# Cluster attention ahead of two expert layers: how ties are broken and who prepares a pair of heads

## The chip, the cores and the metric

The program runs on one core of a Trainium2 chip. The metric is the time of one execution on the device, in microseconds (us); lower is better. Three runs of the kernel before took 713.77 to 715.09 us, with a median of 714.46. The execution that the profiler recorded took 715.44 us, of which 713.6 are the span from the first instruction to the last. TensorE is called PE in the rows (PEld is its weight load), VectorE DVE, ScalarE ACT, GpSimd POOL, and SP is the engine that issues most DMAs.

## The reference

Three layers follow one another: attention with clusters, a layer with a PReLU, and a layer of eight experts. The change touches the first alone:

```python
q_assign = np.argmax(np.einsum('bhsd,hcd->bhsc', q_n, c_n), axis=-1)   # q_n, c_n: normalized
k_assign = np.argmax(np.einsum('bhsd,hcd->bhsc', k_n, c_n), axis=-1)
mask = q_assign[:, :, :, None] == k_assign[:, :, None, :]
scores = scale * np.matmul(q, k.transpose(0, 1, 3, 2))                 # scale = 1/8
scores = np.where(mask, scores, -1000000000.0)
scores = scores - np.max(scores, axis=-1, keepdims=True)
attn = np.exp(scores)
attn = attn / (np.sum(attn, axis=-1, keepdims=True) + 1e-09)
return np.matmul(attn, v).astype(np.float32)
```

There are 2 batches, 8 heads, 768 tokens of 64 numbers, and 16 clusters. `argmax` takes the first of equal maxima. A query sees the keys of its own cluster only.

## The kernel before

Attention goes over eight **pairs** of heads, n = 0 to 7 (four pairs for each batch). A head has six tiles of 128 queries, so a pair is twelve **steps**, k = 0 to 11, and `i = 12n + k` counts all 96. The order of the instructions is written out by hand: the strings `ORD` say for each third step in which order the parts follow, and every engine takes its instructions strictly in that order.

A step has these parts. `scores` (S): four matmuls give 128 x 768 scores; each is a product of a high part (`AB`) and a correction (`CD`), and `CD` also holds the one-hot of the cluster, with 2^60 where the key's cluster is the same, so that the mask is part of the product. `highest` (M): VectorE takes the maximum of each row. `expo` (E): ScalarE computes the exponential and, as a second output, the row's sum into `den`. `transp` (A, B): two steps later TensorE transposes the exponentials, ScalarE copies them as the high part `eth`, and VectorE subtracts for the low part `etl` (a, b). `pv` (P): the product with V, whose high and low parts stand beside each other in `vh`. `evac` (V) takes a finished group of three tiles from PSUM. `X` is one step of a conversion of the next layer's weights, spread over ScalarE (L585, L586), VectorE (L588, L590, L592) and GpSimd (L594); it stands at the steps that `CVX` does not exclude.

The next pair m = n + 1 is prepared inside the steps of pair n, at the end of the step:

- k = 1 and 2: `sims`, twelve small matmuls in all, give the similarity of 128 x 192 query (then key) and cluster values; VectorE takes the maximum (L193) and marks what equals it (L195). Rounding can mark two clusters. To keep the first, GpSimd multiplies the marks by weights 16 to 1 (`weigh`, L202), at k = 3 VectorE takes the maximum again (L211), and GpSimd turns it into one-hots in two instructions (L217, L218).
- k = 2 and 3: `split`, eight instructions of GpSimd, makes the high and low parts of queries and keys (`RL`). k = 6: `place` copies them to `AB` and `CD` by DMA.
- k = 8 (7 for m = 1): `onehots` transposes the one-hots on TensorE (L253), ScalarE copies them (L264, L265), and `placeoh` sends them to `CD` by three DMAs.
- k = 8: `load` of the pair after that; k = 8 and 10: `vsplit` of V, the high part by ScalarE (L246), the low part by GpSimd (L247). k = 11: `scaleq`, GpSimd multiplies the loaded queries by 1/8 (L226). For pair 1 ScalarE does so ahead of the loop (L223).

Every tile that TensorE writes here for transposes, similarities and one-hots comes from one pool of three PSUM buffers (`pt`). `recip` (L387, L388) adds 1e-9 to the sums and inverts them at k = 10 and at k = 1 of the next pair; GpSimd spreads the inverse (`rx`, L391), and TensorE transposes that two steps later (`pb`, L400). The scores' PSUM tile `s` has two buffers, so the scores of step i wait for the exponential of step i - 2.

Ahead of step 0 stands the preparation of pair 0, in its own code, with idle matmuls (`warm`, L141) between.

Of the kernel before, what the change touches and what calls it, by code (L numbers as in the profile page):

```python
# [8 lines left out]
F32 = mybir.dt.float32  # L9
F32R = mybir.dt.float32r  # L10
BF16 = mybir.dt.bfloat16
# [9 lines left out]
P = 128  # L21
B, H, S, D = 2, 8, 768, 64
NC_ = 16
# [70 lines left out]
OK = 8  # L94
CVX = (5, 6, 7, 8, 11)
REST = 4
SIM, SP, S2, VS = (1, 2), (2, 3), 3, (8, 10)
# [3 lines left out]
def attention(ctx, tc, A, cst, xs, Tp, conv=None, prepare=None, then=None):  # L101
# [75 lines left out]

    G = 2 * NT * 2
    halves = [slice(u * 384, (u + 1) * 384) for u in range(2)]

    def sims(n, x):
        b, p = seq[n]
        if x == 0:
            pairs[n] = hk.tile([P, G, NC_], F32, tag="eq", name="eq", bufs=1)
        eq = pairs[n]
        sim = ps_t.tile([P, 512], F32, tag="pt", name="sim")
        for t in range(NT):
            nc.tensor.matmul(sim[:, t * 32:(t + 1) * 32], lhsT=Tp[:, x, t * P:(t + 1) * P],
                             rhs=bd[:, p].rearrange("p j c -> p (j c)"), start=True, stop=True)
        g = G // 2  # L190
        sv = sim[:, :g * NC_].rearrange("p (g c) -> p g c", c=NC_)
        mx = wk.tile([P, g], F32, tag="mx", name="mx")
        nc.vector.tensor_reduce(out=mx, in_=sv, axis=AX.X, op=ALU.max)  # L193
        ex = eq[:, x * g:(x + 1) * g]
        nc.vector.tensor_tensor(out=sv if n == 0 else ex, in0=sv, in1=mx.unsqueeze(2).to_broadcast([P, g, NC_]), op=ALU.is_equal)  # L195
        if n == 0:
            weigh(nc.vector, ex, sv)
        elif x == 1:
            weigh(nc.gpsimd, eq, eq)

    def weigh(eng, out, eq):
        eng.tensor_tensor(out=out, in0=eq, in1=cw.unsqueeze(1).to_broadcast(eq.shape), op=ALU.mult)  # L202

    def sims2(n, xs=(0, 1)):
        eq = pairs[n]
        if xs[0] == 0:
            hots[n] = hk.tile([P, 2, NT, 32], BF16, tag="oh", name="oh", bufs=1)
        g = G // 2
        gs = slice(xs[0] * g, (xs[-1] + 1) * g)
        m2 = wk.tile([P, G], F32, tag="m2", name="m2")  # L210
        nc.vector.tensor_reduce(out=m2[:, gs], in_=eq[:, gs], axis=AX.X, op=ALU.max)  # L211
        oh, mb = hots[n].rearrange("p x t (j c) -> p (x t j) c", c=NC_)[:, gs], m2[:, gs].unsqueeze(2).to_broadcast([P, gs.stop - gs.start, NC_])
        if n == 0:
            nc.vector.tensor_tensor(out=oh, in0=eq[:, gs], in1=mb, op=ALU.is_equal)
        else:

            nc.gpsimd.tensor_tensor(out=eq[:, gs], in0=eq[:, gs], in1=mb, op=ALU.subtract)  # L217
            nc.gpsimd.tensor_scalar(out=oh, in0=eq[:, gs], scalar1=-1.0, scalar2=1.0, op0=ALU.max, op1=ALU.add)  # L218

    def scaleq(n):  # L220
        q = Tp[:, 0]
        if n == 1:
            nc.scalar.mul(q, q, 0.125)  # L223
        else:
            for u in halves:
                nc.gpsimd.tensor_scalar(out=q[:, u], in0=q[:, u], scalar1=0.125, scalar2=None, op0=ALU.mult)  # L226
# [14 lines left out]
    def vsplit(n, j):  # L241
        vt = loads[n]
        vh = wk.tile([P, NT, 2 * D], F32R, tag="vh", name="vh", bufs=4)
        vj = vt[:, j].rearrange("p (t d) -> p t d", d=D)
        h, l = (slice(0, D), slice(D, 2 * D))[::1 - 2 * j]
        nc.scalar.copy(vh[:, :, h], vj)  # L246
        nc.gpsimd.tensor_tensor(out=vh[:, :, l], in0=vj, in1=vh[:, :, h].bitcast(F32), op=ALU.subtract)  # L247
        heads[n, j] = vh
# [7 lines left out]
    def onehots(n):  # L256
        oh = hots.pop(n)
        po = ps_t.tile([P, 512], F32, tag="pt", name="po")
        for x in range(2):
            turn(oh, po, x)  # L260
        pv = po.rearrange("p (x g s) -> p x g s", x=2, g=2)
        st = hk.tile([96, 2, 2, P], F32R, tag="st", name="st", bufs=1)
        heads[n, "st"] = st
        nc.scalar.copy(st[:, 0], pv[:96, 0])  # L264
        nc.scalar.activation(st[:, 1], pv[:96, 1], AF.Copy, bias=-BIG, scale=BIG)  # L265
# [35 lines left out]
    def scores(i):  # L301
# [10 lines left out]
        if t % 3 == 0:  # L312
            if j == 0:
                dens[n, t // 3] = wk.tile([P, 2, 3], F32, tag="den", name="den", bufs=4)
# [12 lines left out]
    def expo(i):  # L327
# [4 lines left out]
                             accum_out=den[:, i % 3:i % 3 + 1])  # L332
# [52 lines left out]
    def recip(n, g):  # L385
        rd = wk.tile([P, 2, 3], F32, tag="rd", name="rd")
        nc.vector.tensor_scalar(out=rd, in0=dens[n, g], scalar1=1e-9, scalar2=None, op0=ALU.add)  # L387
# [58 lines left out]
    nc.gpsimd.memset(CDs[1][D:].bitcast(F32), 0.0)  # L446
    if len(seq) > 1:
        load(1)
        scaleq(1)
# [11 lines left out]
    for i in range(NI + L + 7):  # L461
# [55 lines left out]
        if m < len(seq):  # L517
            if k in SIM:
                sims(m, SIM.index(k))
            if k == S2 and m == 1:  # L520
                sims2(m)
            if k in SP:
                split(m, SP.index(k))
            if k == S2 and m > 1:
                sims2(m)
            if k == 6:
                place(m, 0)
            if k == (OK if m > 1 else OK - 1):
                onehots(m)
                placeoh(m, 0)  # L530
            if k == LK and m + 1 < len(seq):
                load(m + 1)
            if k == VS[0]:
                vsplit(m, 0)
            if k == VS[1]:
                vsplit(m, 1)
            if k == 11 and m + 1 < len(seq):
                scaleq(m + 1)
# [1355 lines left out]
```

## Time and profile before

| | us |
|---|---|
| median of three runs | 714.46 |
| lowest, highest | 713.77, 715.09 |
| profiled execution | 715.44 |
| its span | 713.6 |
| TensorE, share of the span busy | 694.8, 97% |
| VectorE | 573.5, 80% |
| ScalarE | 472.7, 66% |
| GpSimd | 379.0, 53% |

Attention is the first third of the span: the first scores start at 11.8 us, the last exponential at 245.7. Matmuls overlap each other, so a TensorE that reads as 97% busy can still be held up; what tells it apart is the distance from the scores of one step to those of the next.

### The profile page before, as it was taken

What the parts mean: (1) busy time and instruction counts of PE and PEld (TensorE: products, weight loads), DVE (VectorE), ACT (ScalarE), POOL (GpSimd) and SP (SyncE); (2) the same over time, 40 slices, a digit from 0 to 9 for tenths busy, and PEclk for the clock granted to TensorE, in tenths of its full rate; (3) what the DMA queues carried; (4) which work ended last, traced back from release to release, by engine and by line L of the source; (5) the groups of instructions that cost most, each with busy time, mean ns of one, the idle gap of its engine ahead of it and who ended that gap; (6) DMA issues with size and microseconds to landing.
All of it is one profiled execution on the core that took longest, in us unless ns stands there. A gap on an engine that the chain in (4) does not pass through costs nothing.

```text
span 713.6 us, 11822 instructions
## 1 busy us (share of the span) xinstructions
PE 694.8 (97%) x4111; PEld 623.9 (87%) x4111; DVE 573.5 (80%) x1145; ACT 472.7 (66%) x917; POOL 379.0 (53%) x339
## 2 busy tenths in 40 slices
PE   8999999999999999999999999999999999999995
PEld 6988989989999899888889999999888989898883
DVE  6989988898989878887884989977458888787871
ACT  6879788888889964445544655566645767564660
POOL 4649788697886386666663000001024888885101
PEclk9999999999999999999999999999999999999998
DMA  7867676666775133334303600016453999988000
GB/s 200 222 158 170 134 178 153 159 155 135 173 170 107 59 118 118 118 122 133 132 28 117 194 1 1 1 59 180 130 193 103 358 383 354 340 322 324 34 14 25
DMA packets 43905, 108.43 MB, mean 152 GB/s; under 512 B 8698, under 2 KB 24522, under 8 KB 38464
## 3 DMA queue, kind: packets, MB, share of 16 engines
q1 hardware_dynamic: 36768, 67.03, 34.4%
q0 software_dynamic: 7072, 40.60, 15.5%
q8 instruction: 34, 0.56, 0.3%
q14 instruction: 31, 0.25, 0.1%
HBM read 74.78 MB, written 10.10 MB: 119 GB/s over the span
## 4 chain that ended last, share of the span: by engine, by line
PE 68%; DVE 7%; DMA 7%; POOL 6%; ACT 5%; issue 5%; POOLq 0%; ACTq 0%; DVEq 0%
PE h L677 18%; PE y L726 16%; DMA raw<-in_wall_dram,wi 6%; PE yo L1210 6%; PE hw L1288 5%; PE pt L342 4%; PE h L1210 3%; PE s L308 2%; PE px L360 2%; PE y L736 2%; PE s L311 2%; DVE nm L324 2%; ACT e L331 2%; DVE etl L345 2%; PE px L362 2%
## 5 line engine op out<-in xcount | busy, mean ns | idle before, releaser
L345 DVE TENSOR_TENSOR etl<-pt,eth 128x384 fp32r<-128x384 f32 x192 | 102.0, 549 | 19.9 <-ACT eth L344 18.8
L344 ACT CAST eth<-pt 128x384 fp32r<-128x384 f32 x192 | 90.9, 486 | 21.0 <-PE pt L342 20.9
L1177 POOL DMA_INDIRECT xg<-y1d,gi x16 | 27.3, 1708 | 130.2 <-DVE gi L1026 113.8
L342 PE MATMUL pt<-ident,e 128*128 128x128 f32 x576 | 93.8, 273 | 0.3 <-ACT e L331 0.3
L331 ACT ACTIVATE e<-s,nm 128x768 f32<-128x768 f32 x96 | 87.4, 910 | 6.4 <-DVE nm L324 5.7
L324 DVE TENSOR_REDUCE nm<-s 128x1 f32<-128x768 f32 x96 | 90.4, 943 | 1.0 <-PE s L311 0.8
L705 ACT CAST gh<-gm 128x384 fp32r<-128x384 f32 x60 | 30.8, 514 | 81.7 <-DVE gm L703 58.5
L342 PEld LDWEIGHTS pt<-ident,e 128*128 128x128 f32 x576 | 73.7, 140 | 6.9 <-ACT e L331 0.5
L707 DVE TENSOR_TENSOR gl<-gm,gh 128x384 fp32r<-128x384 f32 x60 | 49.3, 822 | 25.7 <-ACT gh L705 25.1
L360 PE MATMUL px<-etl,vh 128*64 128x384 f32 (+1 forms) x192 | 65.7, 369 | 1.6 <-DVE etl L345 1.3
L308 PE MATMUL s<-AB 128*128 128x384 f32 x192 | 57.6, 381 | 2.5 <-ACT e L331 2.0
L577 POOL TENSOR_TENSOR pre<-ct,pre 128x512 int32<-128x512 int32 x26 | 37.2, 1450 | 35.8 <-DVE ct L575 35.8
L677 PE MATMUL h<-xh,wh 128*128 128x384 f32 x256 | 55.6, 338 | 0.6 <-DVE gm L700 0.4
L677 PE MATMUL h<-xh,wl 128*128 128x384 f32 x256 | 56.0, 339 | 0.0
L677 PE MATMUL h<-xl,wh 128*128 128x384 f32 x256 | 55.0, 336 | 0.0
L362 PE MATMUL px<-eth,vh 128*128 128x384 f32 x160 | 54.0, 338 | 0.0
L1612 DVE TENSOR_TENSOR wl<-raw,wh 128x2048 fp32r<-128x2048 f32 (+2 forms) x26 | 44.4, 1714 | 11.2 <-ACT wh L1608 9.8
L311 PE MATMUL s<-CD 128*128 128x384 f32 x192 | 49.2, 337 | 1.1 <-DVE CD L439 1.1
L677 PEld LDWEIGHTS h<-xh,wh 128*128 128x128 f32 x256 | 45.5, 188 | 3.3 <-DVE gm L700 0.5
L677 PEld LDWEIGHTS h<-xh,wl 128*128 128x128 f32 x256 | 44.6, 188 | 2.8 <-POOL wl L649 2.7
L677 PEld LDWEIGHTS h<-xl,wh 128*128 128x128 f32 x256 | 45.7, 188 | 0.0
L726 PE MATMUL y<-wh,gh 128*128 128x512 f32 x168 | 43.6, 394 | 0.0
(383 smaller groups left out, 1826.9 us busy)
## 6 DMA issues: line engine op xcount, KB each, us to landing
AB<-RL SPq DMA_DIRECT2D x31, 384.0 KB, 5.2
raw<-in_w_in_dram SPq DMA_DIRECT2D x16, 512.0 KB, 4.1
raw<-in_w_out_dram SPq DMA_DIRECT2D x16, 512.0 KB, 4.8
raw<-in_wall_dram SPq DMA_DIRECT2D x8, 1024.0 KB, 7.2
Tp<-in_qkT_dram SPq DMA_DIRECT2D x16, 384.0 KB, 3.9
CD<-RL SPq DMA_DIRECT2D x15, 384.0 KB, 7.4
raw<-in_wall_dram POOLq DMA_DIRECT2D x4, 1024.0 KB
vt<-in_v_dram SPq DMA_DIRECT2D x8, 384.0 KB, 6.6
```

The lines of the kernel that those rows point to most:

```text
L308: nc.tensor.matmul(s[:, u, :384], lhsT=AB[:, 0, t * P:(t + 1) * P], rhs=AB[:, 1, ks], start=True, stop=False)
L311: nc.tensor.matmul(s[:, u, :384], lhsT=CD[:, 0, t * P:(t + 1) * P], rhs=CD[:, 1, ks], start=False, stop=True)
L324: nc.vector.tensor_reduce(out=nm, in_=s[:, :, :384], axis=AX.XY, op=ALU.max, negate=True)
L331: nc.scalar.activation(e.rearrange("p (u c) -> p u c", u=2), s[:, :, :384], AF.Exp, bias=nm, accum_out=den[:, i % 3:i % 3 + 1])
L342: nc.tensor.transpose(pt[:, i2], e[:, kt * P:(kt + 1) * P], ident)
L344: nc.scalar.copy(eh, pt)
L345: lows[u] = lambda: nc.vector.tensor_tensor(out=etl[:, 3 * u:3 * u + 3, q * P:(q + 1) * P], in0=pt, in1=eh.bitcast(F32), op=ALU.subtract)
L360: nc.tensor.matmul(px[:m], lhsT=vh[:, kt, :m], rhs=etl[:, kt], start=False, stop=False)
L362: nc.tensor.matmul(px, lhsT=vh[:, kt, :], rhs=eth[:, kt], start=False, stop=(kt == NT - 1))
L677: nc.tensor.matmul(hs[c], lhsT=a[:, k * P:(k + 1) * P], rhs=x[:, k, c * HC:(c + 1) * HC], start=(k == 0 and i == 0), stop=(k == KD - 1 and ...
L726: nc.tensor.matmul(ys[gi * GT + t], lhsT=a[:, t * P:(t + 1) * P], rhs=w, start=(f == 0 and n == 0), stop=(gi == 0 and f == NF - 1 and n == 2))
L1210: nc.tensor.matmul(out, lhsT=l[:, k], rhs=r[:, k * DM:(k + 1) * DM], start=start and k == 0 and i == 0, stop=stop and k == 3 and i == len( ...
```

## The change

It has four parts. (1) Ties: the marks of all equal maxima go straight into the one-hot tile as bf16 (L200 now), and are transposed as they are at k = 3 (`equals`); VectorE copies them from PSUM to `eqt`. At k = 4 (`onehots`) one product for queries and one for keys with a constant matrix `clear` subtracts, for each cluster, the marks of the clusters ahead of it; what is above 0 is the first mark. ScalarE takes it for the queries (`Relu`), VectorE for the keys. The four instructions of `weigh` and `sims2` go, for all pairs but the first. `placeoh` moves to k = 6, ahead of `place`. (2) V's high part is made by GpSimd with an addition of zero, and `vsplit` of the first head moves from k = 8 to k = 1. (3) The queries are scaled behind the similarities, at k = 1, by a `tensor_tensor` with a tile that holds 1/8, for pair 1 too. (4) The sums lie in four fixed tiles, each sum beside a column that holds 1e-9; `recip` adds the two columns with a `tensor_reduce`. These tiles, 1/8 and `clear` are filled by GpSimd ahead of step 0.

```diff
--- before.py
+++ after.py
@@ -91,10 +91,10 @@
 LATE = 3
 WARM = (8, 3, 4, 9, 6)
 PREP = (33, 45)
-OK = 8
+OK = 4
 CVX = (5, 6, 7, 8, 11)
 REST = 4
-SIM, SP, S2, VS = (1, 2), (2, 3), 3, (8, 10)
+SIM, SP, EQ, VS = (1, 2), (2, 3), 3, (1, 10)
 ORD = ("SMAPXaBbE", "SMAPaVBXEb", "SAPXBMabE")
 
 
@@ -175,14 +175,19 @@
         CDs.append(cd)
     nc.gpsimd.memset(CDs[0][D:].bitcast(F32), 0.0)
 
+    sums = [hk.tile([P, 2, 3, 2], F32, name=f"den{i}") for i in range(4)]
+    eighth = one.tile([P, 1], F32, name="eighth")
+    clear = one.tile([96, 2, 96], BF16, name="clear")
+
     G = 2 * NT * 2
     halves = [slice(u * 384, (u + 1) * 384) for u in range(2)]
 
     def sims(n, x):
         b, p = seq[n]
+        if x == 0 and n == 0:
+            pairs[n] = hk.tile([P, G, NC_], F32, tag="eq", name="eq", bufs=1)
         if x == 0:
-            pairs[n] = hk.tile([P, G, NC_], F32, tag="eq", name="eq", bufs=1)
-        eq = pairs[n]
+            hots[n] = hk.tile([P, 2, NT, 32], BF16, tag="oh", name="oh", bufs=1)
         sim = ps_t.tile([P, 512], F32, tag="pt", name="sim")
         for t in range(NT):
             nc.tensor.matmul(sim[:, t * 32:(t + 1) * 32], lhsT=Tp[:, x, t * P:(t + 1) * P],
@@ -191,39 +196,23 @@
         sv = sim[:, :g * NC_].rearrange("p (g c) -> p g c", c=NC_)
         mx = wk.tile([P, g], F32, tag="mx", name="mx")
         nc.vector.tensor_reduce(out=mx, in_=sv, axis=AX.X, op=ALU.max)
-        ex = eq[:, x * g:(x + 1) * g]
-        nc.vector.tensor_tensor(out=sv if n == 0 else ex, in0=sv, in1=mx.unsqueeze(2).to_broadcast([P, g, NC_]), op=ALU.is_equal)
+        eq = sv if n == 0 else hots[n][:, x].rearrange("p t (j c) -> p (t j) c", c=NC_)
+        nc.vector.tensor_tensor(out=eq, in0=sv, in1=mx.unsqueeze(2).to_broadcast([P, g, NC_]), op=ALU.is_equal)
         if n == 0:
-            weigh(nc.vector, ex, sv)
-        elif x == 1:
-            weigh(nc.gpsimd, eq, eq)
-
-    def weigh(eng, out, eq):
-        eng.tensor_tensor(out=out, in0=eq, in1=cw.unsqueeze(1).to_broadcast(eq.shape), op=ALU.mult)
+            nc.vector.tensor_tensor(out=pairs[n][:, x * g:(x + 1) * g], in0=sv, in1=cw.unsqueeze(1).to_broadcast(sv.shape), op=ALU.mult)
 
     def sims2(n, xs=(0, 1)):
         eq = pairs[n]
-        if xs[0] == 0:
-            hots[n] = hk.tile([P, 2, NT, 32], BF16, tag="oh", name="oh", bufs=1)
         g = G // 2
         gs = slice(xs[0] * g, (xs[-1] + 1) * g)
         m2 = wk.tile([P, G], F32, tag="m2", name="m2")
         nc.vector.tensor_reduce(out=m2[:, gs], in_=eq[:, gs], axis=AX.X, op=ALU.max)
         oh, mb = hots[n].rearrange("p x t (j c) -> p (x t j) c", c=NC_)[:, gs], m2[:, gs].unsqueeze(2).to_broadcast([P, gs.stop - gs.start, NC_])
-        if n == 0:
-            nc.vector.tensor_tensor(out=oh, in0=eq[:, gs], in1=mb, op=ALU.is_equal)
-        else:
-
-            nc.gpsimd.tensor_tensor(out=eq[:, gs], in0=eq[:, gs], in1=mb, op=ALU.subtract)
-            nc.gpsimd.tensor_scalar(out=oh, in0=eq[:, gs], scalar1=-1.0, scalar2=1.0, op0=ALU.max, op1=ALU.add)
+        nc.vector.tensor_tensor(out=oh, in0=eq[:, gs], in1=mb, op=ALU.is_equal)
 
     def scaleq(n):
-        q = Tp[:, 0]
-        if n == 1:
-            nc.scalar.mul(q, q, 0.125)
-        else:
-            for u in halves:
-                nc.gpsimd.tensor_scalar(out=q[:, u], in0=q[:, u], scalar1=0.125, scalar2=None, op0=ALU.mult)
+        for u in halves:
+            nc.gpsimd.tensor_tensor(out=Tp[:, 0, u], in0=Tp[:, 0, u], in1=eighth.to_broadcast([P, S // 2]), op=ALU.mult)
 
     def split(n, part):
         if part == 0:
@@ -243,7 +232,10 @@
         vh = wk.tile([P, NT, 2 * D], F32R, tag="vh", name="vh", bufs=4)
         vj = vt[:, j].rearrange("p (t d) -> p t d", d=D)
         h, l = (slice(0, D), slice(D, 2 * D))[::1 - 2 * j]
-        nc.scalar.copy(vh[:, :, h], vj)
+        if n:
+            nc.gpsimd.tensor_tensor(out=vh[:, :, h], in0=vj, in1=zero.unsqueeze(2).to_broadcast([P, NT, D]), op=ALU.add)
+        else:
+            nc.scalar.copy(vh[:, :, h], vj)
         nc.gpsimd.tensor_tensor(out=vh[:, :, l], in0=vj, in1=vh[:, :, h].bitcast(F32), op=ALU.subtract)
         heads[n, j] = vh
 
@@ -253,16 +245,25 @@
             nc.tensor.matmul(po[:96, (2 * x + g) * P:(2 * x + g + 1) * P], lhsT=oh[:, x, 3 * g:3 * g + 3].rearrange("p t c -> p (t c)"),
                              rhs=identb, start=True, stop=True)
 
-    def onehots(n):
+    def equals(n):
         oh = hots.pop(n)
         po = ps_t.tile([P, 512], F32, tag="pt", name="po")
         for x in range(2):
             turn(oh, po, x)
-        pv = po.rearrange("p (x g s) -> p x g s", x=2, g=2)
+        eqt = hots[n] = hk.tile([96, 2, 2 * P], BF16, tag="eqt", name="eqt", bufs=1)
+        nc.vector.tensor_copy(eqt, po[:96].rearrange("p (x s) -> p x s", x=2))
+
+    def onehots(n):
+
+        eqt = hots.pop(n)
+        po = ps_t.tile([P, 2, 2 * P], F32, tag="pt", name="po")
+        for x in range(2):
+            nc.tensor.matmul(po[:96, x], lhsT=clear[:, x], rhs=eqt[:, x], start=True, stop=True)
+        pv = po.rearrange("p x (g s) -> p x g s", g=2)
         st = hk.tile([96, 2, 2, P], F32R, tag="st", name="st", bufs=1)
         heads[n, "st"] = st
-        nc.scalar.copy(st[:, 0], pv[:96, 0])
-        nc.scalar.activation(st[:, 1], pv[:96, 1], AF.Copy, bias=-BIG, scale=BIG)
+        nc.scalar.activation(st[:, 0], pv[:96, 0], AF.Relu)
+        nc.vector.tensor_scalar(out=st[:, 1], in0=pv[:96, 1], scalar1=0.0, scalar2=-BIG, op0=ALU.max, op1=ALU.add)
 
     def onehot0(x):
 
@@ -311,7 +312,7 @@
             nc.tensor.matmul(s[:, u, :384], lhsT=CD[:, 0, t * P:(t + 1) * P], rhs=CD[:, 1, ks], start=False, stop=True)
         if t % 3 == 0:
             if j == 0:
-                dens[n, t // 3] = wk.tile([P, 2, 3], F32, tag="den", name="den", bufs=4)
+                dens[n, t // 3] = sums[2 * (n % 2) + t // 3]
             den = dens[n, t // 3][:, j]
             eth = wk.tile([P, NT, 384], F32R, tag="eth", name="eth", bufs=2)
             etl = wk.tile([P, NT, 384], F32R, tag="etl", name="etl", bufs=2)
@@ -329,7 +330,7 @@
         den = grp[i // 3][0]
         e = es.pop("e") if i == 0 else wk.tile([P, S], F32, tag="e", name="e", bufs=3)
         nc.scalar.activation(e.rearrange("p (u c) -> p u c", u=2), s[:, :, :384], AF.Exp, bias=nm,
-                             accum_out=den[:, i % 3:i % 3 + 1])
+                             accum_out=den[:, i % 3, :1])
         es[i] = e
 
     def transp(i, u):
@@ -384,7 +385,7 @@
 
     def recip(n, g):
         rd = wk.tile([P, 2, 3], F32, tag="rd", name="rd")
-        nc.vector.tensor_scalar(out=rd, in0=dens[n, g], scalar1=1e-9, scalar2=None, op0=ALU.add)
+        nc.vector.tensor_reduce(out=rd, in_=dens[n, g], axis=AX.X, op=ALU.add)
         nc.vector.reciprocal(out=rd, in_=rd)
         rx = wk.tile([P, 3, 2, D], F32, tag="rx", name="rx", bufs=1)
         eng = nc.gpsimd if n < len(seq) - 1 else nc.vector
@@ -444,9 +445,19 @@
     vsplit(0, 0)
     vsplit(0, 1)
     nc.gpsimd.memset(CDs[1][D:].bitcast(F32), 0.0)
+    nc.gpsimd.memset(eighth, 0.125)
+
+    cq, ck = clear[:, 0], clear[:, 1]
+    nc.gpsimd.memset(cq, -1.0)
+    cb = cq.rearrange("p (b c) -> p b c", c=NC_)
+    nc.gpsimd.affine_select(out=cb, in_=cb, compare_op=ALU.is_gt, fill=0.0, base=0, pattern=[[NC_, 6], [1, NC_]], channel_multiplier=-1)
+    nc.gpsimd.affine_select(out=cb, in_=cb, compare_op=ALU.is_ge, fill=0.0, base=0, pattern=[[-NC_, 6], [0, NC_]], channel_multiplier=1)
+    nc.gpsimd.tensor_tensor(out=cq, in0=cq, in1=identb[:96, :96], op=ALU.add)
+    nc.gpsimd.tensor_scalar(out=ck, in0=cq, scalar1=BIG, scalar2=None, op0=ALU.mult)
+    for d in sums:
+        nc.gpsimd.memset(d, 1e-9)
     if len(seq) > 1:
         load(1)
-        scaleq(1)
 
     def before():
         for f in range(3):
@@ -515,27 +526,25 @@
             if spare and i > NI + NRM:
                 spare.pop(0)()
         if m < len(seq):
+            if k == VS[0]:
+                vsplit(m, 0)
             if k in SIM:
                 sims(m, SIM.index(k))
-            if k == S2 and m == 1:
-                sims2(m)
+            if k == SIM[0]:
+                scaleq(m)
             if k in SP:
                 split(m, SP.index(k))
-            if k == S2 and m > 1:
-                sims2(m)
+            if k == EQ:
+                equals(m)
+            if k == OK:
+                onehots(m)
             if k == 6:
+                placeoh(m, 0)
                 place(m, 0)
-            if k == (OK if m > 1 else OK - 1):
-                onehots(m)
-                placeoh(m, 0)
             if k == LK and m + 1 < len(seq):
                 load(m + 1)
-            if k == VS[0]:
-                vsplit(m, 0)
             if k == VS[1]:
                 vsplit(m, 1)
-            if k == 11 and m + 1 < len(seq):
-                scaleq(m + 1)
     for do in spare:
         do()
     return fill
```

On GpSimd, between the preparation of pair 0 and that of pair 1, stood before (`vh` is V's parts of pair 0, `CD_168` a zero that pair 0 needs at k = 6, the rest is pair 1):

```order
L247 TENSOR_TENSOR vh<-vt,vh 128x6x64 x2
L446 MEMSET CD_168 64x1536
L202 TENSOR_TENSOR eq<-eq,cw 128x384
L234 TENSOR_TENSOR RL<-Tp,zero 128x384 x4
L217 TENSOR_TENSOR eq<-eq,m_366 128x384
L218 TENSOR_SCALAR oh<-eq 128x384
```

and at the same place after (`den_170` to `den_173` are the tiles of the sums):

```order
L239 TENSOR_TENSOR vh<-vt,vh 128x6x64 x2
L447 MEMSET CD_168 64x1536
L448 MEMSET eighth 128x1
L451 MEMSET clear 96x96
L453 AFFINE_SELECT clear<-clear 96x96
L454 AFFINE_SELECT clear<-clear 96x96
L455 TENSOR_TENSOR clear<-clear,identb 96x96
L456 TENSOR_SCALAR clear<-clear 96x96
L458 MEMSET den_170 128x12
L458 MEMSET den_171 128x12
L236 TENSOR_TENSOR vh<-vt,zero 128x6x64
L239 TENSOR_TENSOR vh<-vt,vh 128x6x64
```

The tiles of the sums are filled behind two passes over V, one large memset and six instructions for the constants.

On ScalarE, steps 7 to 10 of pair 2, before:

```order
L331 ACTIVATE e,den<-s,nm 128x768
L264 CAST st<-po 96x256
L265 ACTIVATE st<-po 96x256
L246 CAST vh<-vt 128x6x64
L344 CAST eth<-pt 128x3x128
L585 ACTIVATE w32a<-raw_78 128x256
L586 ACTIVATE raw_78<-raw_78 128x256
L344 CAST eth<-pt 128x3x128
L331 ACTIVATE e,den<-s,nm 128x768
```

and the same stretch after:

```order
L332 ACTIVATE e,den_170<-s,nm 128x768
L345 CAST eth<-pt 128x3x128
L594 ACTIVATE w32a<-raw_78 128x256
L595 ACTIVATE raw_78<-raw_78 128x256
L345 CAST eth<-pt 128x3x128
L332 ACTIVATE e,den_171<-s,nm 128x768
```

Three instructions between two exponentials are gone; the exponential now names the fixed tile of its sum.

On TensorE, a step before has the four transposes of one-hots alone (here step 7 of pair 0):

```order
L342 MATMUL pt<-ident,e 128x128 x3
L253 LDWEIGHTS oh
L253 MATMUL po<-identb,oh 96x128
L253 LDWEIGHTS oh
L253 MATMUL po<-identb,oh 96x128
L253 LDWEIGHTS oh
L253 MATMUL po<-identb,oh 96x128
L253 LDWEIGHTS oh
L253 MATMUL po<-identb,oh 96x128
L308 MATMUL s<-AB_167 128x384 x2
```

After, steps 3 and 4 of pair 0 (the tail of the transposes, then the product one step later):

```order
L245 LDWEIGHTS oh
L245 MATMUL po<-identb,oh 96x128
L309 MATMUL s<-AB_165 128x384 x2
L312 MATMUL s<-CD_166 128x384 x2
L343 MATMUL pt<-ident,e 128x128 x6
L261 LDWEIGHTS clear
L261 MATMUL po<-eqt,clear 96x256
L261 LDWEIGHTS clear
L261 MATMUL po<-eqt,clear 96x256
L309 MATMUL s<-AB_165 128x384 x2
```

The same transposes stand four or five steps earlier, and two matmuls of 256 columns are added between the transposes of one step and the scores of the next.

## Rows read from the trace of the kernel before

**Rows 1.** The page, busy time by engine: us (share of the span) instructions

```profile
PE 694.8 (97%) x4111; PEld 623.9 (87%) x4111; DVE 573.5 (80%) x1145; ACT 472.7 (66%) x917; POOL 379.0 (53%) x339
```

**Rows 2.** Timeline, TensorE, scores of a step: start, duration (us), engine, line, [idle before]

```profile
39.44 0.60 PE L308 MATMUL s<-AB 128*128 128x384 f32 x2
44.63 0.59 PE L308 MATMUL s<-AB 128*128 128x384 f32 x2
...
93.33 0.60 PE L308 MATMUL s<-AB 128*128 128x384 f32 x2
96.08 0.62 PE L308 MATMUL s<-AB 128*128 128x384 f32 x2 [0.43 <-ACT e L331]
...
147.03 0.61 PE L308 MATMUL s<-AB 128*128 128x384 f32 x2
149.11 0.60 PE L308 MATMUL s<-AB 128*128 128x384 f32 x2
...
151.45 0.59 PE L308 MATMUL s<-AB 128*128 128x384 f32 x2
155.56 0.60 PE L308 MATMUL s<-AB 128*128 128x384 f32 x2
158.50 0.59 PE L308 MATMUL s<-AB 128*128 128x384 f32 x2
```

**Rows 3.** Timeline, GpSimd, start of the kernel

```profile
1.00 0.29 POOL masks.py:199 TENSOR_SCALAR_AFFINE_SELECT ident<-ident 128x128 f32<-128x128 f32 x1
...
12.50 2.71 POOL L247 TENSOR_TENSOR vh<-vt,vh 128x384 fp32r<-128x384 f32 x2 [3.92 <-ACT vh L246]
15.27 1.38 POOL L446 MEMSET CD<- 64x1536 f32 x1
```

**Rows 4.** Timeline, TensorE and ScalarE, the first two exponentials and scores behind them

```profile
14.65 1.42 PE L188 MATMUL sim<-bd,Tp 128*128 128x32 f32 x12
15.14 0.90 ACT L331 ACTIVATE e<-s,nm 128x768 f32<-128x768 f32 x1 [1.56 <-DVE nm L324]
...
16.19 0.62 PE L308 MATMUL s<-AB 128*128 128x384 f32 x2
```

**Rows 5.** Timeline, ScalarE, step 8 of pair 2

```profile
92.80 0.39 ACT L265 ACTIVATE st<-po 96x256 fp32r<-96x256 f32 x1
93.08 0.52 ACT L246 CAST vh<-vt 128x384 fp32r<-128x384 f32 x1
...
93.85 0.45 ACT L585 ACTIVATE w32a<-raw 128x256 int32<-128x256 uint16 x1
```

**Rows 6.** Lines L387, L211: VectorE, times, duration ns min/median/max, first and last start

```profile
L387 DVE TENSOR_SCALAR rd<-den x16: 151/223/935, 34.3 to 248.9; 128x6 f32<-128x6 f32 x16
...
L211 DVE TENSOR_REDUCE m<-eq x9: 353/541/543, 8.1 to 201.5; 128x24 f32<-128x384 f32 x7, 128x12 f32<-128x192 f32 x2
```

**Rows 7.** Groups by form, 100 to 240 us: busy us, mean ns | idle before

```profile
L387 DVE TENSOR_SCALAR rd<-den 128x6 f32<-128x6 f32 x9 | 3.4, 376 | 0.0
...
L594 POOL TENSOR_TENSOR w32a<-raw,w32a 128x256 int32<-128x256 int32 x5 | 3.7, 744 | 1.1 <-DVE raw L592 1.1
```

**Rows 8.** Timeline, VectorE, one-hots of pair 0 from PSUM

```profile
13.41 0.42 DVE L442 CAST st<-po 96x256 fp32r<-96x256 f32 x1
```

**Rows 9.** Waits of the weight load, 20 to 245 us: total us, times, longest

```profile
PEld s L308 <- ACT e L331: 4.8, 10, 0.7
PEld px L360 <- DVE etl L345: 3.7, 9, 0.9
PEld sim L188 <- POOL Tp L226: 1.7, 2, 1.3
PEld pb L400 <- POOL rx L391: 0.9, 2, 0.4
```

**Rows 10.** Timeline, TensorE, warm matmuls, early and later

```profile
1.50 2.44 PE L141 MATMUL warm<-warm 128*128 128x384 bf16 x7
...
9.09 1.63 PE L141 MATMUL warm<-warm 128*128 128x384 bf16 x9
```

## The prediction, made before the changed kernel ran

> **What bounds the kernel now.** I read the page first: TensorE is busy for 97% of the span, VectorE for 80%, ScalarE for 66%, GpSimd for 53% [rows 1]. A busy TensorE may still be held up, so I went on to the distances between the scores of successive steps in TensorE's timeline. An undisturbed step lasts 149.11 - 147.03 = 2.08 us; one with the four transposes of one-hots lasts 151.45 - 149.11 = 2.34 [rows 2]. That is TensorE's own rhythm: nothing that another engine saves makes such a step shorter. Other steps are longer, and the waits of the weight load between 20 and 245 us say on whom they wait: 4.8 us on exponentials, 3.7 on low parts, 1.7 on the scaled queries, 0.9 on the inverted sums, 11.1 in all [rows 9]. So relief of the other engines is worth some 11 us at the very most, while each instruction added to TensorE, and each wait put into its chain, counts in full. The later layers are not touched; I take it that they begin earlier or later by what attention gains or loses.
>
> **The first exponential gets a new wait.** It writes its sum into a fixed tile, and GpSimd fills that tile first. In the order of GpSimd the fill stands behind V's low parts of pair 0, which end at 12.50 + 2.71 = 15.21, behind the memset from 15.27 to 16.65 [rows 3], and behind six instructions for the constants. The first exponential starts at 15.14 now, and waits for VectorE alone [rows 4]. Of the six, the trace shows a select over 128 columns at 0.29 [rows 3] and an addition over 256 columns at 0.74 [rows 7]. I take 0.29 for each of the two selects, 0.4 for the addition and for the scaling of 96 columns (nearer to the small row), 0.1 to 0.2 for each of the three small fills, 0.4 together, and for five dependent starts the 0.06 that lies between 15.21 and 15.27: 0.58 + 0.8 + 0.4 + 0.3 = 2.1. The tile is filled at 18.7, and the exponential starts 3.6 us later than now. Below, with 0.29 for the four larger ones and nothing for the rest, it is 16.65 + 1.16 - 15.14 = 2.7; above, with 0.74 for the addition and the scaling, 0.29 for five and 0.36 of gaps, 4.8.
>
> Behind that exponential ScalarE holds the second one and all copies of the transposed tiles; TensorE's scores of step 2 need its PSUM buffer and start at 16.19 for that reason, 0.12 after the similarities end at 14.65 + 1.42 [rows 4]. Nothing hides the wait: behind those scores follow transposes, the second similarities and the scores of step 3, all on TensorE in order, with no slack to give the time back. VectorE and GpSimd may run ahead in it, but they aren't the bound. I count +3.6.
>
> **The product that breaks ties.** The four transposes only move from step 8 to step 3. Two matmuls of 256 columns are added for each of seven pairs. The trace has no such product; its nearest row is the four transposes of 128 columns, 512 columns for 2.34 - 2.08 = 0.26 us [rows 2]. The two products pass 512 columns too: 7 x 0.26 = +1.8. With half as many weights to load it may be half of that, 0.9; if the array waits once more for each, twice, 3.6. They wait for VectorE's copy of the transposes, with a whole step between.
>
> **What goes.** (a) The similarities of a pair no longer wait for scaled queries: 1.7 us [rows 9], nearly all in step 1 of pair 1, which lasts 44.63 - 39.44 = 5.19 where 2.08 + 1.42 would do [rows 2, 4]. Late next would be the load, which is issued five steps earlier: -1.7. (b) GpSimd has less in its queue ahead of the spread of the inverted sums, since the two instructions of the ties and one `vsplit` are gone from there, and its remaining work starts two steps earlier; of the two waits of 0.9 in all [rows 9] I count -0.6 (0 to 0.9). (c) At step 8 ScalarE had two copies of one-hots and V's high part, 0.39 + 0.52 and a first of about the same as the 0.39, in front of the conversion's 0.45 [rows 5]; the step from 93.33 to 96.08 lasts 2.75 for it, 0.67 too long [rows 2], and pair 6 has one more such step: -1.3. Where no conversion falls there, the same copies cost nothing today. (d) The addition of 1e-9 has six numbers in a row and takes 151 ns at best and 935 at worst, while a reduction from SBUF over 384 columns takes 541 to 543 at every time [rows 6]: the one is held up while GpSimd works, the other isn't. Nine additions take 3.4 us where 9 x 0.15 would be 1.4 [rows 7], so they lose 2.0 us between 100 and 240, and in pair 4 the whole of it lands in a step of 158.50 - 155.56 = 2.94, 0.86 too long [rows 2]. Over all pairs I count -1.8 (0 to -3). The Trainium skill (GPSIMD Engine Reference, Key points) says that GpSimd shares its SBUF interfaces with VectorE and that instructions in a two-port mode contend; by that rule the reduction is free of it, and the sum keeps its 1.8; were the hold-up due to something else, the sum would be 1.8 higher. The two rows agree with the rule. Together (a) to (d): -5.4.
>
> **What crowds steps 3 to 5.** VectorE's copy of 512 columns replaces a reduction of 0.54 [rows 6] at the same place; 256 columns take 0.42 [rows 8], so 512 about 0.7. At step 4 VectorE gets 0.4 more and ScalarE 0.4. In steps without a conversion ScalarE absorbs three times that at step 8. Where a conversion falls into steps 3 to 5, in four pairs, the exponential is late already, and 0.3 comes on top: +1.2 (0 to 4). What GpSimd gains or loses elsewhere lies beside TensorE.
>
> **The sum.** 3.6 + 1.8 - 5.4 + 1.2 = +1.2 us on the profiled execution of 715.44, so 716.6. That execution is 0.98 over the median of the runs, 714.46, so I expect 715.7. What a measurement of this kernel can tell from no change is about 0.2%, 1.43 us: same means 713.0 to 715.9. The forecast lies inside, near its upper edge. Its own range is 713.7 to 717.3, from the bounds of the start and of what goes.
>
> **Rivals.** *The relief carries further.* ScalarE loses three instructions in each pair, and all waits for exponentials and low parts melt, not only those that I can name. The weight load waits a little ahead of the matmuls, so of its 11.1 us I take 9 as lost to TensorE; if all go, the sum is 3.6 + 1.8 - 9 = -3.6, 710.9; with half of the remaining ones, 712.5. For it: three of four kinds of waits lead to engines that get relief. Against it: the conversion's instructions stay, and most waits for exponentials stand behind them.
>
> *The gap lowers the clock.* Between 16.07 and about 19.8 TensorE would have nothing to do, 3.7 us. At the start of the kernel the warm matmuls follow each other every 0.32 us, later every 0.16 [rows 10], the two levels of 1.2 and 2.4 GHz for 384 columns. The low level is there from 1.50 to 3.94 at least and over by 9.09. If it came back for as long, 2.4 to 7.6 us, half of that is lost: about +2.5, 718.2. Against it: nothing in the trace of before shows a fall in mid-kernel. The Trainium skill (TensorE: Matmul & The Clock Gate, What's actually happening) has the clock fall back to its lower level behind idle time; by it this gap is the one place where that could happen. No row here shows it either way.
>
> *Steps 3 and 4 become the bound (slower).* The product needs VectorE's copy, and its results need ScalarE and VectorE again, out of the same three PSUM buffers as the transposes. If either engine can't make up 0.4 us within one step, TensorE waits once in each of six pairs for about the 0.67 of the step above: 4.0 instead of 1.2, so 718.5. It decides from the point where a step 4 lasts over 2.34 + 0.3.
>
> *The column of the sums doesn't help.* The reduction is held up like the addition: the 1.8 is missing, 717.5.
>
> **How the numbers follow.** Forecast 0.50, of which 0.05 is faster, 0.30 the same, 0.15 slower. Relief carries further 0.20 (faster 0.18, same 0.02). Clock 0.13, all slower. Steps 3 and 4, 0.10 (slower 0.09, same 0.01). Column 0.07 (slower 0.06, same 0.01). So faster 0.23, same 0.34, slower 0.43. The range of eight in ten goes from 712.3, inside the relief's case, to 718.8, beyond the clock's and the crowding's.
>
> **What would show it.** Right: the first exponential starts between 17.8 and 20, released by GpSimd; scores of step 2 follow a microsecond later; step 1 of pair 1 lasts about 3.5; step 8 lasts 2.08 in every pair; the sums' reduction takes under 0.25 us each time; step 4 is longer by 0.26. Wrong: a first exponential at 15.2, warm-like spacing of matmuls doubled behind 19 us, steps 4 and 5 over 2.6 in pairs without a conversion, or a stall of similarities on a DMA.

## The result, and the profile after

The changed kernel took 721.92 us (median of four: 719.22 to 722.94), the kernel before 714.22 in the same session: a ratio of 1.0080 [1.0055, 1.0105]. Predicted were 715.7 and at most 718.8. It is slower by more than was forecast, and outside the range.

The execution that was profiled is the shortest of the four, 719.22 (span 717.4). Against that of before, 715.44, it is 3.8 longer, where the sum said 1.2. All of it lies in attention: the first scores start at 11.77 in both, those of the last step at 241.96 before and at 245.79 now.

The timeline at the start, GpSimd and ScalarE and then TensorE (start, duration, engine, line, tiles, [idle before <- what ended it]); it answers to [rows 3, 4]:

```profile
15.27 1.37 POOL L447 MEMSET CD<- 64x1536 f32 x1
...
16.99 0.30 POOL L453 TENSOR_SCALAR_AFFINE_SELECT clear<-clear 96x96 bf16<-96x96 bf16 x1
17.36 0.30 POOL L454 TENSOR_SCALAR_AFFINE_SELECT clear<-clear 96x96 bf16<-96x96 bf16 x1
17.74 0.36 POOL L455 TENSOR_TENSOR clear<-clear,identb 96x96 bf16<-96x96 bf16 x1
18.20 0.49 POOL L456 TENSOR_SCALAR clear<-clear 96x96 bf16<-96x96 bf16 x1
18.74 0.24 POOL L458 MEMSET den<- 128x12 f32 x4
...
18.89 0.90 ACT L332 ACTIVATE e<-s,nm 128x768 f32<-128x768 f32 x1 [6.05 <-POOL den L458]
```
```profile
14.65 1.42 PE L193 MATMUL sim<-bd,Tp 128*128 128x32 f32 x12
19.93 1.01 PE L309 MATMUL s<-AB 128*128 128x384 f32 x2 [3.87 <-ACT e L332]
20.74 0.84 PE L312 MATMUL s<-CD 128*128 128x384 f32 x2
21.38 1.48 PE L343 MATMUL pt<-ident,e 128*128 128x128 f32 x6
22.65 1.57 PE L193 MATMUL sim<-bd,Tp 128*128 128x32 f32 x12
24.05 0.60 PE L309 MATMUL s<-AB 128*128 128x384 f32 x2
```

The exponential waits for GpSimd's filling of the sums, as forecast, and TensorE stands 3.87 us. What was not in the sum is in the durations behind the gap: the scores take 1.01 and the six transposes 1.48 us, and once it is over 0.60 and 0.82. The windows of the same execution (length, busy us of each engine, then PEclk, the granted clock as a share) say why:

```profile
0.00:19.50 19.50, 13.58 (x79) 9.31 (x79) 10.76 (x28) 10.03 (x19) 10.92 (x25) 1.00 0.76 205
19.50:23.00 3.50, 3.07 (x13) 2.97 (x13) 1.19 (x2) 1.84 (x6) 3.42 (x5) 0.51 0.97 290
23.00:40.00 17.00, 16.71 (x117) 15.21 (x117) 15.69 (x29) 14.26 (x33) 6.40 (x8) 1.00 0.60 153
```

For some 3.5 us behind the idle time TensorE has the lower of its two levels, 1.2 GHz for 2.4. Step 2 of the first pair lasts 24.05 - 19.93 = 4.12 for it; in the kernel before it lasted 18.91 - 16.19 = 2.72, with 16.19 from [rows 4] and this line of the same timeline:

```profile
18.91 0.60 PE L308 MATMUL s<-AB 128*128 128x384 f32 x2
```

The second thing that was not in the sum is step 3. Its scores start at 81.77 and those of the next step at 84.88 in pair 2, 3.11 apart, where before the step lasted 2.38 to 2.41, and the four transposes that moved there take 0.27. First the two scores of before, then the end of the step after:

```profile
77.62 0.60 PE L308 MATMUL s<-AB 128*128 128x384 f32 x2
...
80.01 0.60 PE L308 MATMUL s<-AB 128*128 128x384 f32 x2
```

```profile
83.58 0.49 PE L401 MATMUL pb<-ident,rx 128*128 128x128 f32 x3
83.90 0.49 PE L343 MATMUL pt<-ident,e 128*128 128x128 f32 x3
84.69 0.38 PE L245 MATMUL po<-identb,oh 128*96 128x128 bf16 x4 [0.29 <-ACT rb L402]
84.88 0.60 PE L309 MATMUL s<-AB 128*128 128x384 f32 x2
```

The waits of TensorE and of its weight load from 20 to 250 us (total, times, longest) show it once in each of six pairs. Before had no such rows:

```profile
PE s L309 <- ACT e L332: 4.2, 2, 3.9
PE po L245 <- ACT rb L402: 1.7, 6, 0.3
PEld L245 <- issue: 2.6, 6, 0.4
```

The third row is the weight load of the same transposes, which stands 0.4 each time; `issue` says that the profile names no releaser for it.

The reliefs came. The similarities of pair 1 no longer wait (scores at 44.99 and 48.60, 3.61 apart, where [rows 2] have 5.19); the steps that lasted 2.75 and 2.94 there last 99.66 - 97.56 = 2.10 and 161.29 - 159.22 = 2.07; and the sums' reduction, by line, is as long at every time, where [rows 6] have 151 to 935 ns:

```profile
L388 DVE TENSOR_REDUCE rd<-den x16: 153/156/159, 39.7 to 252.7; 128x6 f32<-128x12 f32 x16
```

### The profile page after: what moved, and what is told of

Same layout as the page of the kernel before. It is cut to its first block, busy times and chain, and to the rows that moved or that the text cites. A ratio compares the mean times of both kernels' runs of the same rounds, so it can differ in the third digit from the quotient of the medians.

```text
span 717.4 us, 11842 instructions
## 1 busy us (share of the span) xinstructions
PE 697.4 (97%) x4125; PEld 626.1 (87%) x4125; DVE 574.5 (80%) x1152; ACT 466.8 (65%) x895; POOL 366.9 (51%) x344
## 4 chain that ended last, share of the span: by engine, by line
PE 78%; DMA 6%; DVE 6%; ACT 4%; issue 3%; POOL 1%; POOLq 0%; DVEq 0%; ACTq 0%
PE h L686 18%; PE y L735 16%; PE pt L343 7%; DMA raw<-in_wall_dram,wi 6%; PE yo L1219 6%; PE hw L1297 5%; PE s L309 4%; PE px L361 4%; PE s L312 4%; PE px L363 3%; PE h L1219 3%; PE sim L193 2%; PE y L745 2%; DVE etl L346 1%; DVE nm L325 1%
```

## The experiments

Ratios are to the kernel before, timed in the same session; they rest on all executions and are not the quotient of the two medians. The diffs are excerpts: what else an edit needs is left out. The median of the kernel before was 715.05 (32 executions, 713.66 to 718.33) beside the first four experiments and 714.84 (29, 713.53 to 717.72) beside the last four.

| experiment | median us | lowest | ratio [95%] |
|---|---|---|---|
| early_fill | 717.12 | 713.53 | 0.9999 [0.9981, 1.0017] |
| early_eq4 | 712.52 | 711.15 | 0.9961 [0.9945, 0.9977] |
| warm_gap | 718.67 | 717.10 | 1.0048 [1.0028, 1.0067] |
| before_sums | 712.83 | 712.07 | 0.9957 [0.9942, 0.9973] |
| after_again | 722.09 | 718.92 | 1.0094 [1.0060, 1.0128] |
| before_late | 717.86 | 714.49 | 1.0037 [1.0018, 1.0055] |
| scale_behind | 713.75 | 712.73 | 0.9989 [0.9974, 1.0004] |
| eq4_scalar | 713.96 | 712.34 | 0.9987 [0.9968, 1.0005] |

In some executions TensorE's matmuls stay slow for longer ahead of the first scores, which start at 14.93 to 15.11 in the profiled executions of early_fill, early_eq4 and before_sums, and at 11.45 to 13.03 in the others. That makes some 3 us; a median carries some of it, so the lowest and the lengths of steps are read beside it.

**early_fill: the wait.** The changed kernel with the sums filled ahead of GpSimd's other work (the same two lines go from behind the constants):

```diff
     sums = [hk.tile([P, 2, 3, 2], F32, name=f"den{i}") for i in range(4)]
+    for d in sums:
+        nc.gpsimd.memset(d, 1e-9)
```

> The changed kernel with one move: GpSimd fills the four tiles of the sums right behind its first memset, 15 us ahead of their use; all else as changed. Theory of the start (the first exponential waits 3.7 us for the fill, and TensorE's gap of 3.9 us brings the lower clock, 1.4 us in the profiled execution and more in the others): the first exponential starts at 15.1 again, no stretch at the lower level, and the time falls from 721.9 to between 712.5 and 714.2. Rival (the loss lies in the steps, by the product that breaks ties and GpSimd's new work): it falls by the 3.7 at most and stays at 717 or above.

It took 4.8 us less than the changed kernel by medians, 5.7 by the lowest. The median is above the forecast's 712.5 to 714.2 and as high as the rival has it: seven of the twelve executions took 717.03 to 717.51, five 713.53 to 715.20. The profiled one is of the seven, with its first scores at 15.11 for 11.77, so the lengths of steps decide. The scores of steps 1 and 2 start at 17.19 and 19.49: step 1 of the first pair lasts 2.30 in place of 5.98, and no low clock follows:

```profile
17.19 0.51 PE L311 MATMUL s<-AB 128*128 128x384 f32 x2
...
19.49 0.62 PE L311 MATMUL s<-AB 128*128 128x384 f32 x2 [0.18 <-ACT e L334]
```
```profile
16.00:21.00 5.00, 4.05 (x30) 3.93 (x30) 4.41 (x8) 2.13 (x6) 4.66 (x8) 1.00 0.61 140
```

Step 3 stays at 3.06 to 3.12. So the late fill cost more than its wait of 3.75, and without it the change is worth nothing.

**early_eq4: the three buffers.** early_fill with transposes and product of the ties one step later:

```diff
-OK = 4
+OK = 5
-SIM, SP, EQ, VS = (1, 2), (2, 3), 3, (1, 10)
+SIM, SP, EQ, VS = (1, 2), (2, 3), 4, (1, 10)
```

> As the run before it, with the transposes of the marks at step 4 instead of 3 and the product at step 5 instead of 4. Theory of the buffers (at step 3 four groups want the three PSUM buffers, since the inverted sums are transposed there too, so TensorE waits 0.46 us in each pair): step 3 goes back to 2.38 us, step 4 lasts 2.34, step 5 about 2.28, and 2.8 us go: 710 to 711.5. Rival (VectorE's copy of 512 columns, 0.68 us, is late for whatever comes behind it): the 0.46 us turn up at step 4 or 5, and the time is that of the run before it.

4.6 less than early_fill by medians, 2.4 by the lowest; the median is above the forecast's 710 to 711.5, while the steps came as forecast. The transposes have no wait left among TensorE's, and step 3 ends after 2.40 (78.53 to 80.93 in pair 2) and step 4 after 2.33:

```profile
78.53 0.60 PE L311 MATMUL s<-AB 128*128 128x384 f32 x2
...
80.93 0.59 PE L311 MATMUL s<-AB 128*128 128x384 f32 x2
...
83.06 0.39 PE L247 MATMUL po<-identb,oh 128*96 128x128 bf16 x4
83.26 0.60 PE L311 MATMUL s<-AB 128*128 128x384 f32 x2
```

The transposes (0.27 at step 4) and the product (0.22 at step 5) are paid, but not the wait: 6 x 0.46 = 2.8 us are back. At step 3 the inverted sums (`pb`), both halves of the exponentials (`pt`) and the transposes (`po`) want three buffers, and `po` gets its own when ScalarE's copy of `pb` ends. At step 4 there is no `pb`. This version beats both kernels (ratio 0.9961 to the kernel before).

**warm_gap: the clock alone.** The changed kernel, with idle matmuls in the gap. The wait stays:

```diff
+        if i == 1:
+            busy(22)
```

> The changed kernel with 22 warm matmuls of 384 columns (0.16 us each) behind the similarities of step 1, so that TensorE works through the gap in which it waits for the first exponential; the wait itself stays. Theory of the clock: the first exponential still starts at 18.9, the clock stays at its upper level until the kernel's end, the time is 717.3 to 718.3 and its runs lie within 1.5 us of each other. Rival (the clock has no part in it, and the spread of the runs from 719 to 723 has another cause): 721 to 722 with the same spread.

3.3 us less than the changed kernel by medians, 2.1 by the lowest. The median is 0.4 above the forecast, and the executions spread over 4.3 us where it said 1.5: five of the twelve took 720.90 to 721.44, and why isn't shown. The windows from 16 to 30 us have the upper level throughout, and the timeline has the same wait with short matmuls behind it:

```profile
16.00:21.00 5.00, 4.86 (x35) 3.18 (x33) 1.89 (x4) 0.92 (x3) 4.47 (x13) 1.00 0.66 149
21.00:30.00 9.00, 8.57 (x61) 7.57 (x62) 7.30 (x14) 7.01 (x17) 8.96 (x11) 1.00 0.68 237
```
```profile
17.12 3.74 PE L141 MATMUL warm<-warm 128*128 128x384 bf16 x22
21.13 0.62 PE L309 MATMUL s<-AB 128*128 128x384 f32 x2 [0.27 <-ACT e L332]
...
21.95 0.82 PE L343 MATMUL pt<-ident,e 128*128 128x128 f32 x6
...
23.86 0.60 PE L309 MATMUL s<-AB 128*128 128x384 f32 x2
```

Step 1 lasts 5.98 as in the changed kernel and step 2 lasts 2.73 for 4.12. So idleness of TensorE brought the low clock, not the wait of ScalarE or GpSimd's work.

**before_sums: part 4 alone**, on the kernel before, filled early:

```diff
-        nc.vector.tensor_scalar(out=rd, in0=dens[n, g], scalar1=1e-9, scalar2=None, op0=ALU.add)
+        nc.vector.tensor_reduce(out=rd, in_=dens[n, g], axis=AX.X, op=ALU.add)
```

> The kernel before with the fourth part of the change alone: sums beside a column of 1e-9 in fixed tiles, filled early, added by a reduction. Theory of the shared interface (the addition was held up while GpSimd worked, the reduction isn't): the reduction takes 0.16 us each time, the long steps 11 shrink, and the time falls by 1.8 to 2.2 to about 712.2. Rival (the time gained on VectorE is not on TensorE's path): 714.2, no change.

2.2 us less than the kernel before by medians, 1.6 by the lowest. The step of [rows 2] that lasted 2.94 lasts 158.47 - 156.30 = 2.17, and the reduction 146 to 156 ns. Term (d) stands by itself. How long the addition is held up depends on the moment, though: in scale_behind below, which keeps it, the addition at step 11 of pair 2 takes 0.16 us for 0.74 in the kernel before, and that step 2.18 for 2.76. So 0.6 of the 2.2 that the table below counts for (d) can also come without the reduction.

**after_again: what spreads the times.** The changed kernel, unaltered.

> The changed kernel itself, unaltered, to see what spreads its times (719.2 to 722.9). If the stretch at the lower clock behind the gap differs from execution to execution, the executions with a lower mean granted clock take longer, about 0.3 to 0.4 us for each us at the lower clock: 719 at a mean of 0.994, 723 at 0.986. If it is only the late rise of the clock ahead of the first scores (the other cause of spread seen so far, about 3.2 us), the times fall into two groups that the mean clock does not tell apart. Median 719 to 723 in both.

Mean granted clock and time go together in eight of the kernel's ten executions: 0.994 at 718.92 to 719.41, 0.989 at 721.29 and 721.37, 0.987 and 0.986 at 722.55 to 722.94. Two do not fit: with 0.989 and 0.988 they took 724.88 and 725.26, some 3 us more; late first scores make as much, but neither was profiled. The execution of 722.81 was profiled, and its windows and timeline are:

```profile
17.80:31.50 13.70, 10.95 (x47) 10.64 (x48) 6.41 (x10) 5.98 (x13) 11.84 (x20) 0.50 0.53 173
31.50:50.00 18.50, 18.50 (x127) 17.57 (x126) 16.08 (x28) 16.53 (x40) 2.30 (x3) 1.00 0.72 168
```
```profile
20.55 1.01 PE L309 MATMUL s<-AB 128*128 128x384 f32 x2 [3.86 <-ACT e L332]
...
25.70 0.99 PE L309 MATMUL s<-AB 128*128 128x384 f32 x2
...
28.79 0.99 PE L309 MATMUL s<-AB 128*128 128x384 f32 x2
```

The gap is the same, 3.86, but the lower level lasts to 31.5. The first pair lasts 33.66 here, 30.82 in the execution of 719.22, 29.39 in warm_gap and 25.60 in early_fill: the wait is worth 3.8, a short fall of the clock 1.4 and a long one 4.3. By their means of 0.986 to 0.989, three of the first four executions had a longer fall than the profiled one.

**before_late: half the gap, on the kernel before.** Part 4 alone, filled behind GpSimd's clearing:

```diff
     nc.gpsimd.memset(CDs[1][D:].bitcast(F32), 0.0)
+    for d in sums:
+        nc.gpsimd.memset(d, 1e-9)
```

> The kernel before with part 4 alone (the column of sums), but the four tiles filled where the change fills them, behind GpSimd's clearing of the correction's rows. GpSimd is free at 16.65 there, so the first exponential should start at about 17.0 instead of 15.14, and the scores of step 2 at 18.0 instead of 16.19: a gap of about 1.9 us behind the similarities, half of the changed kernel's 3.9. By the wait alone: +1.9 against the same part with the early fill, 714.7 by medians. If the clock falls behind a gap of this length too, matmuls behind it are spaced double for some us and the time is 1.4 to 4 us higher still, 716 to 719. If a wait of the first exponential costs nothing (scores catch up), 712.8.

717.86, 5.0 above before_sums (in another session), inside the forecast for a falling clock. TensorE stands 1.81 us, and the clock fell:

```profile
17.57 0.62 PE L310 MATMUL s<-AB 128*128 128x384 f32 x2 [1.81 <-ACT e L333]
...
19.68 2.61 PE L190 MATMUL sim<-bd,Tp 128*128 128x32 f32 x12
22.10 0.99 PE L310 MATMUL s<-AB 128*128 128x384 f32 x2
```
```profile
18.50:25.00 6.50, 6.50 (x30) 6.40 (x29) 3.83 (x7) 2.33 (x5) 1.85 (x3) 0.50 0.97 308
```

The first pair is 4.6 longer than before's: 1.7 of it is the wait, 3.0 lie in steps 2 and 3, at the low clock. A gap of half the length thus brought a fall that cost more than its wait. Part of it is given back: step 1 of pair 1 is 1.56 shorter, since the scaled queries, late there in the kernel before, are now in time for a later TensorE.

**scale_behind: part 3 alone**, on the kernel before, still with `tensor_scalar`:

```diff
+            if k == SIM[0]:
+                scaleq(m)
-            if k == 11 and m + 1 < len(seq):
-                scaleq(m + 1)
```

> The kernel before with part 3 alone: queries scaled by GpSimd behind their similarities in step 1, for pair 1 too. By the prediction's term (a) the similarities of pair 1 no longer wait, step 1 of the first pair falls from 5.2 to about 3.5, and the time by 1.7 to 1.9, to about 713.1 by medians. If the similarities then wait for the load instead, nothing is gained; if GpSimd's two instructions of 1.2 us each delay its high parts and one-hots behind them until step 6 or 8 is late, it is slower.

By the clock 1.1 us less, and the interval still reaches no change; by the trace the mechanism is there. Step 1 of pair 1 lasts 43.69 - 40.08 = 3.61, and among the weight load's waits the similarities' for GpSimd ([rows 9], 1.7 us) is gone. No other step got longer by more than 0.05. The term is worth 1.6 in the profiled execution and about 1 over all. Not every execution of the kernel before needs to have this wait: in before_sums, which scales the queries as that kernel does, the first scores start at 15.06, and step 1 of pair 1 lasts 46.33 - 42.70 = 3.63 too.

**eq4_scalar: V's high parts back on ScalarE**, and those of the first head at step 8 again, from early_eq4:

```diff
-SIM, SP, EQ, VS = (1, 2), (2, 3), 4, (1, 10)
+SIM, SP, EQ, VS = (1, 2), (2, 3), 4, (8, 10)
-        if n:
-            nc.gpsimd.tensor_tensor(out=vh[:, :, h], in0=vj, in1=zero.unsqueeze(2).to_broadcast([P, NT, D]), op=ALU.add)
-        else:
-            nc.scalar.copy(vh[:, :, h], vj)
+        nc.scalar.copy(vh[:, :, h], vj)
```

> The changed kernel with the early fill and the ties a step later (transposes at step 4, product at step 5), and V's high parts on ScalarE at steps 8 and 10 as before. By the prediction's term (c) ScalarE is late again at step 8 where a conversion falls there: up to +1.3 against the same kernel with GpSimd's additions, 713.8 by medians; but the one-hots' copies are gone from step 8 here, so a part of it may stay won, +0.3 to +0.8. If V's move to GpSimd costs more than it gives, since GpSimd spreads the inverted sums in the same steps, it is faster, below 712.

1.4 more than early_eq4 by medians, 1.2 by the lowest; the two ran in different sessions, so this is less sure than the rest. The forecast's size came, not quite its place. The step of [rows 2] behind step 9 of pair 2 that lasted 2.75 lasts 95.17 - 92.66 = 2.51 here and 2.10 in early_eq4, so two thirds of that delay are V's and the rest, by elimination, the one-hots'. Another delay lies at step 5 of pair 2, 2.74 for 2.29 in early_eq4, and isn't explained: ScalarE has the product's result there in both.

## Why the prediction was wrong, point by point

| term, us | forecast | measured, by steps of the profiled executions |
|---|---|---|
| start: wait of the first exponential | +3.6 | +3.75 |
| clock behind the gap | 0 (rival, 0.13) | +1.4, and +4.3 in a longer execution |
| product for ties | +1.8 | 7 steps x 0.20 to 0.25 = +1.5 |
| crowding of steps 3 to 5 | +1.2 | 6 x 0.46 = +2.8 |
| (a) similarities | -1.7 | -1.9 |
| (b) inverted sums | -0.6 | -0.6 |
| (c) ScalarE's copies | -1.3 | -1.3 |
| (d) addition of the sums | -1.8 | -2.2 |
| last pair | 0 | +0.7 |
| sum | +1.2 | +4.15 |

The terms add up to 0.3 more than the 3.8 measured; what is left lies in steps that no term names.

The step that failed is the choice against the rival *the gap lowers the clock*: the sum put the clock at nothing. The forecast computed the gap itself rightly (3.7 for 3.87) and priced the rival at +2.5, between the 1.4 and the 4.3 measured, but gave it 0.13, since "nothing in the trace of before shows a fall in mid-kernel", and "No row here shows it either way". That trace has no such gap in mid-kernel, so its silence there was no evidence. At its end it does show a fall: TensorE's last matmul is over at 704.31 + 1.10 = 705.41, and the granted clock goes from 1.00 to 0.50 while the engine stands idle. These are lines of the timeline and the windows of before:

```profile
704.31 1.10 PE L1210 MATMUL yo<-wh,hT 128*128 128x512 f32 x4
```
```profile
705.50:709.00 3.50, 0.00 (x0) 0.00 (x0) 0.70 (x1) 0.00 (x0) 0.98 (x1) 1.00 0.22 82
709.00:713.60 4.60, 0.00 (x0) 0.00 (x0) 0.00 (x0) 0.00 (x0) 0.00 (x0) 0.50 0.00 2
```

So a row for the rival stood in the trace that the prediction was made from. The sign that it named for this case, matmuls at doubled spacing behind 19 us, is what came. The Trainium skill's rule (TensorE: Matmul & The Clock Gate, What's actually happening), that the clock falls to its lower level behind idle time, is what happened in every profiled execution with the gap, at 0.51 and 0.50 of full speed; warm_gap, which fills it, kept 1.00.

The second is the term *what crowds steps 3 to 5*, mis-sized. It was worked out from what VectorE and ScalarE have to do, as 0.3 in four pairs. What decides is the buffers: three for `pb`, two `pt` and `po`, and a wait that comes in all six pairs, whatever the conversion does. The rival *steps 3 and 4 become the bound* named these buffers and had 4.0 for them, near the 2.8 of this step; its test was step 4, which kept within bounds (2.56 at most for 2.64), while the wait stands at step 3.

Right were the place, size and releaser of the first wait, the price of the product, which lies by the transposes' and not by its two waits, and all four reliefs, -6.0 for -5.4. Of its other signs one failed: step 8 of pair 3 lasts 2.41, not 2.08. The rule on the shared SBUF interfaces (the Trainium skill, GPSIMD Engine Reference, Key points) bears on (d), and the reduction's 153 to 159 ns agree with it.

In the median, which is 2.7 above the profiled execution, the clock weighs more than in the table, as most executions have, by their mean clock, a longer fall. The reliefs are read against an execution of before of 715.44 that is over its median, and not every execution has all of them: scale_behind brings 1.1 for a wait of 1.6. Open is the 0.7 of the last pair, one step of which lasts 2.70 for 2.05. It lasts 2.58 to 2.77 in every kernel with the new ties, 2.05 with part 3 alone, and 2.08 and 2.33 with part 4 alone; no experiment was aimed at it.

## What to carry to other kernels

An instruction that fills a constant costs its queue's position, not its duration: four fills of 0.24 us together, issued behind other set-up from 15.27 to 18.74, held the first exponential for 3.75, and early_fill got that back by moving two lines. Price a gap on TensorE with what the clock does behind it, and fill it with idle matmuls if it can't be closed. When a step gains a PSUM tile, count the tiles of the pool that are live in that step and who frees them; one step further the same work can come without the wait.

## What the runs showed of the hardware

A gap of the same length (3.87 and 3.86 us) was followed by the lower clock for about 3.5 us in one execution and about 13.7 in another of the same kernel, so the cost of a gap isn't one number. A fall can come without a long gap too: in eq4_scalar, with the early fill, the clock is low around 15.8 to 19.2 (0.56 by the window), and step 2 of its first pair lasts 20.01 - 15.96 = 4.05. The longest idle time of TensorE ahead of it within the loop is 1.11 us; the kernel before has the same 1.11 at that place and no fall:

```profile
15.80:19.20 3.40, 3.40 (x16) 3.23 (x17) 2.07 (x4) 1.74 (x6) 2.94 (x8) 0.56 0.95 214
```
```profile
13.24 0.58 PE L311 MATMUL s<-CD 128*128 128x384 f32 x2 [1.11 <-DVE CD L439]
...
15.96 1.01 PE L308 MATMUL s<-AB 128*128 128x384 f32 x2
...
20.01 0.59 PE L308 MATMUL s<-AB 128*128 128x384 f32 x2
```

And at the start TensorE gets fast early in some executions and late in others, with nothing changed that bears on it: the 24 similarities of pair 0 took 3.09 us in the profiled execution of before and 5.17 in that of early_fill, where the first scores start at 15.11 for 11.77. The granted clock reads 1.00 in both stretches, so there the length of the matmuls is the only sign of the lower level. What decides between the two wasn't found.
